# A retention layer with a SoLU feed-forward layer: steps of 256 tokens and four heads, attention on 64x64 tiles, and a fixed order for every engine

## The chip, the cores and the metric

The kernel runs on one core of one Trainium2 chip. The metric is the device time of one execution in microseconds (us), the median of several runs, each kernel measured in turn with the kernel before on the same chip. Ratios are the mean time of one kernel's fast runs divided by the mean time of the fast runs of the kernel before in the same rounds, so they are not quite the ratio of the medians that are quoted beside them. "Span" is the time from the first to the last instruction in a profiled execution; it is some 2 us shorter than the run's time for most kernels here.

Engine names: PE is the matrix engine, DVE the vector engine, ACT the scalar engine, POOL the third element-wise engine, SP the engine that issues most DMA transfers.

## The reference

Shortened to what is computed:

```python
def _attn_ref(q, k, v):                        # q, k, v: (8 batches, 8 heads, 576 tokens, 64) float32
    scores = (1 / sqrt(64)) * q @ k.T
    gamma = 1.0 - 2.0 ** (-5.0 - arange(8))    # one decay per head
    Dmat = where(rel >= 0, gamma ** rel, 0)    # rel = query position - key position
    return (scores * Dmat) @ v

def _moe_ref(x, w_in, w_out, g_ln):            # x: (4608 tokens, 512), w_in (512, 1024), w_out (1024, 512)
    h = x @ w_in
    solu = h * softmax(h)
    ln = (solu - mean) / sqrt(var + 1e-06) * g_ln
    return ln @ w_out
```

There is no softmax in the attention, so it can be computed as a recurrence: within a chunk of 128 tokens the masked scores are formed, and what earlier chunks contribute goes through a 64x64 state for each head. The 4608 tokens are 36 chunks of 128.

## The kernel before

Each of 36 steps takes one chunk of 128 tokens and all eight heads. The parts that the change touches:

```python
def load(i):                       # q, k, v: one token per partition
    ...
    nc.sync.dma_start(out=t, in_=src[b, :, c * P : (c + 1) * P, :].rearrange("h p d -> p h d"))

def qk_tp(i):                      # 8 transpositions of 128x128 into ONE PSUM bank (tqk)
    ...
def scores(i):                     # 8 matmuls, 64 rows x 128 columns, two at a time
    for hp in range(4):
        for e in range(2):
            dd = slice(e * 64, e * 64 + 64)
            nc.tensor.matmul(out=s_ps[:, e, hp], lhsT=qkT[dd, 1, hp], rhs=qkT[dd, 0, hp], ...)
def kv_mm(i):                      # 8 matmuls, 128 rows x 64 columns: new state
    ...
def inter(i):                      # 4 matmuls 128x128: query times the old state
    ...
def av(i):                         # 8 matmuls, 128 rows x 64 columns: scores times v
    ...
def mm1(i):                        # 8 matmuls: h = x @ w_in, two PSUM banks, one buffer
    ...
def mm2(i):                        # 8 matmuls: o = ln @ w_out, one PSUM bank, one buffer
    ...
for i in range(-LEAD, NS + LAG):   # one hand-written software pipeline; order of issue = order of this text
    a = i + LEAD
    load(i + 6) ...
    state(a - 1); mask(a - 1); stats(i - 1); cast_v(a + 1); scale_qk(a + 1); rstd(i - 1)
    mm1(i); exp_(i); solu(i)
    qk_tp(a); qk_ev(a)
    mm2(i - LAG); o_ev(i - LAG)
    ln_tp(i - 1); ln_ev(i - 1)     # 8 transpositions into the SAME bank as tqk (tln)
    inter(a - 1); scores(a); av(a - 1); x_ev(a - 1); kv_mm(a)
    if i == -1: prep_w_in(); keep_warm(WARM1)
    if 0 <= i < LAG: prep_w2(i)    # w_out times g_ln, minus its column mean
```

Names in the profile: `h_ps` is the output of mm1, `o_ps` of mm2, `s_ps` of the scores, `tqk` and `tln` the transpositions, `e_sb` of the exponential, `solu` of the product h times exp(h), `w2g` and `w2c` the steps of w_out's preparation. I count the mm1 groups from 0 to 35.

The softmax here doesn't subtract the row's maximum and nothing guards it: scores larger than these inputs give would overflow.

## Time and profile before

Three runs gave 246.12 us (245.96 to 247.88).

| what | value | where it is read |
|---|---|---|
| first mm1 (0) starts, its second half starts | 20.84, 24.88 us | timeline of PE |
| mm1 5 starts | 60.69 us | timeline of PE |
| mean period of mm1, steps 10 to 30 | 5.498 us | timeline of PE |
| mm1 35 (the last) to the end | 19.8 us | timeline of PE, span |
| span | 243.4 us | page |

The overview of the kernel before, its span cut into 40 slices of 6.1 us; a digit is the busy share in tenths, and the fourth line counts the DMA packets:

```profile
PE   8375485779999999999999999999999999999861
DMA  8999999990889887979888978797788762111123
GB/s 167 218 367 218 263 292 219 184 209 28 178 192 196 191 209 160 224 157 206 189 197 181 212 160 213 175 240 175 174 205 193 172 169 46 43 46 74 57 86 86
DMA packets 120922, 42.42 MB, mean 174 GB/s; under 512 B 114624, under 2 KB 114752, under 8 KB 120896
```

For the first nine slices PE is idle for about a third of the time while the DMA engines are full, at only 167 to 367 GB/s; from the tenth slice to the end PE is full. Part 3 of the page of the kernel before gives the loads' queue (packets, MB, share of the 16 engines' span):

```profile
q1 hardware_dynamic: 120464, 41.96, 76.5%
```

So there are three stages with different limits: a start of 60 us, a steady stage bound by PE, and a tail. The busy time by window of the kernel before (columns: window, its length, then busy us of PE, PE's weight loads, DVE, ACT, POOL, the granted PE clock, the DMA share, GB/s) says the same:

```profile
core 0: us, PE busy (x) PEld busy (x) DVE busy (x) ACT busy (x) POOL busy (x), PEclk, DMA share, GB/s
0.00:20.00 20.00, 13.37 (x107) 6.98 (x108) 6.53 (x13) 7.20 (x11) 9.28 (x20) 0.75 1.13 245
20.00:40.00 20.00, 11.47 (x104) 5.77 (x103) 11.31 (x18) 9.73 (x17) 10.68 (x17) 0.91 1.15 257
60.00:200.00 140.00, 139.66 (x1491) 82.92 (x1488) 116.76 (x176) 103.24 (x152) 109.29 (x192) 1.00 0.84 191
```

In 140 us of the steady stage PE lacks 0.3 us; the other engines have 17 to 26% to spare. There a gain has to come out of PE's own time. One steady step on PE in the kernel before (columns: start, length, engine, line, operation, output and inputs, tile, shape, count):

```profile
128.75 1.89 PE L344 MATMUL o_ps<-w2c_105,lnT 128*128 128x512 f16 x8
130.57 0.61 PE L329 MATMUL tln<-ident,solu 128*128 128x128 f16 x8
131.01 0.39 PE L255 MATMUL av_ps<-qkT,sbd_109 128*128 128x128 f16 x4
131.33 0.40 PE L191 MATMUL s_ps<-qkT 64*128 64x128 f16 x8
131.66 0.41 PE L267 MATMUL av_ps<-ret,v_1975 128*64 128x128 f16 x8
131.90 0.29 PE L217 MATMUL kv<-v_2089,k_2092 128*64 128x64 f16 x8
132.13 1.90 PE L285 MATMUL h_ps<-w_in_103,xT 128*128 128x512 f16 x8
```

The ends that the profile gives overlap the next start (130.64 against 130.57 in the first two lines), so one reads the distances between starts. From the 128*128 tiles to the scores' 64*128, from there to 128*64, and from there back to 128*128 the tile mode changes: three changes a step.

The start, the first mm1 groups on PE in the kernel before (in brackets: how long PE had been idle just before, and what ended that):

```profile
20.84 1.03 PE L285 MATMUL h_ps<-w_in_103,xT 128*128 128x512 f16 x4
24.88 1.38 PE L285 MATMUL h_ps<-w_in_103,xT 128*128 128x512 f16 x4 [3.01 <-DVE w_in_103 L371]
```

The second half of the first mm1 waits 3.01 us for a cast of w_in on DVE. And the end, the last eviction of an output tile and the issue of its stores, in the timeline of the kernel before:

```profile
238.63 0.69 ACT L352 ACTIVATE o_sb<-o_ps,rs 128x512 f32<-128x512 f32 x1 [2.11 <-PE o_ps L344]
239.34 1.11 SPq L360 DMA_DIRECT2D out_dram<-o_sb  x2
```

### The profile page before, as it was taken

How to read it: one execution, taken by the hardware profiler on the slowest of the kernel's cores; microseconds unless marked ns; L12 is line 12 of the kernel's file. 1: busy time of each engine (PE TensorE's matmuls, PEld its weight loads, DVE VectorE, ACT ScalarE, POOL GpSimd, SP SyncE). 2: the span in 40 equal slices, each digit the busy share in tenths (PEclk: the TensorE clock that was granted, in tenths of full speed). 3: DMA queues.
4: the chain of work that ended last, by engine and by line, in shares of the span. 5: the costliest groups of instructions: out<-in, count | busy, mean ns of one | idle time of the engine just before them, and what ended most of it. 6: DMA issues, size and time to landing. Idle time of an engine off the chain costs nothing.

```text
span 243.4 us, 5629 instructions
## 1 busy us (share of the span) xinstructions
PE 215.8 (89%) x2138; PEld 123.6 (51%) x2138; DVE 174.1 (72%) x266; ACT 156.7 (64%) x230; POOL 155.0 (64%) x277
## 2 busy tenths in 40 slices
PE   8375485779999999999999999999999999999861
PEld 2252233445555655566555655565655555554420
DVE  1450777599979888977798889887888898876400
ACT  2143557547666777777776777777776677766631
POOL 8243575176957888788578887886678878721200
PEclk9858979989999999999999999999999999999998
DMA  8999999990889887979888978797788762111123
GB/s 167 218 367 218 263 292 219 184 209 28 178 192 196 191 209 160 224 157 206 189 197 181 212 160 213 175 240 175 174 205 193 172 169 46 43 46 74 57 86 86
DMA packets 120922, 42.42 MB, mean 174 GB/s; under 512 B 114624, under 2 KB 114752, under 8 KB 120896
## 3 DMA queue, kind: packets, MB, share of 16 engines
q1 hardware_dynamic: 120464, 41.96, 76.5%
q8 instruction: 16, 0.26, 0.5%
q10 hardware_dynamic: 432, 0.12, 0.2%
q14 instruction: 10, 0.08, 0.1%
HBM read 32.63 MB, written 9.44 MB: 173 GB/s over the span
## 4 chain that ended last, share of the span: by engine, by line
PE 73%; SPq 10%; DVE 7%; ACT 5%; DMA 2%; issue 1%; ACTq 0%
PE h_ps L285 25%; PE o_ps L344 24%; SPq L94 7%; PE tln L329 7%; PE tqk L173 5%; PE av_ps L267 4%; PE s_ps L191 4%; PE av_ps L255 2%; DVE solu L301 2%; DVE w2c_105 L386 2%; DMA w_f<-in_moe_w_out_dram 2%; ACT w2g_104 L374 2%; ACT o_sb L352 1%; PE kv L217 1%; ACT e_sb L295 1%
## 5 line engine op out<-in xcount | busy, mean ns | idle before, releaser
L285 PE MATMUL h_ps<-w_in_103,xT 128*128 128x512 f16 x288 | 71.2, 389 | 3.6 <-DVE w_in_103 L371 3.0
L344 PE MATMUL o_ps<-w2c_105,lnT 128*128 128x512 f16 x288 | 68.0, 379 | 2.8 <-ACT o_sb L352 2.8
L295 ACT ACTIVATE e_sb<-h_ps 128x1024 f32<-128x1024 f32 x36 | 36.8, 1023 | 49.6 <-PE h_ps L285 49.6
L301 DVE TENSOR_TENSOR solu<-h_ps,e_sb 128x1024 f16<-128x1024 f32 x36 | 43.7, 1215 | 9.2 <-ACT e_sb L295 9.2
L309 DVE BATCH_NORM_STATS2 bs<-solu 128x6 f32<-128x512 f16 x72 | 45.9, 680 | 0.1
L202 DVE TENSOR_TENSOR ret<-s_ps,masks 128x1024 f16<-128x1024 f32 x36 | 43.7, 1215 | 2.1 <-PE s_ps L191 2.1
L285 PEld LDWEIGHTS <-xT 128*128 128x128 f16 x288 | 26.1, 99 | 34.3 <-issue 8.3
L344 PEld LDWEIGHTS <-lnT 128*128 128x128 f16 x288 | 26.9, 98 | 30.0 <-issue 3.6
L181 ACT COPY qkT<-tqk 128x1024 f16<-128x1024 f16 x36 | 36.1, 1004 | 8.1 <-PE tqk L173 8.1
L337 ACT COPY lnT<-tln 128x1024 f16<-128x1024 f16 x36 | 36.1, 1004 | 2.1 <-PE tln L329 2.1
L352 ACT ACTIVATE o_sb<-o_ps,rs 128x512 f32<-128x512 f32 x36 | 24.7, 687 | 17.3 <-PE o_ps L344 13.9
L237 POOL TENSOR_TENSOR gt<-tt,small 128x256 f32<-128x256 f32 x24 | 14.7, 613 | 26.0 <-DVE tt L236 26.0
L329 PEld LDWEIGHTS <-solu 128*128 128x128 f16 x288 | 19.0, 97 | 15.8 <-issue 11.5
L329 PE MATMUL tln<-ident,solu 128*128 128x128 f16 x288 | 21.8, 218 | 5.0 <-ACT qkT L181 5.0
L276 ACT CAST xT<-av_ps 128x512 f16<-128x512 f32 x36 | 21.5, 596 | 3.4 <-PE av_ps L267 3.4
L236 DVE TENSOR_TENSOR tt<-kv,gt 128x256 f32<-128x256 f32 x24 | 10.1, 422 | 15.4 <-PE kv L217 8.9
L191 PE MATMUL s_ps<-qkT 64*128 64x128 f16 x288 | 14.7, 223 | 4.3 <-ACT qkT L181 4.3
L318 POOL TENSOR_SCALAR w<-se 128x1 f32<-128x1 f32 x36 | 10.3, 285 | 4.8 <-ACT e_sb L295 1.5
L191 PEld LDWEIGHTS <-qkT 64*128 64x128 f16 x288 | 8.3, 96 | 8.4 <-ACT qkT L181 5.2
L242 POOL CAST sbd_109<-gt 64x256 f16<-64x256 f32 x8 | 3.1, 394 | 10.2 <-DVE gt L233 9.9
L233 DVE TENSOR_TENSOR gt<-kv,small 128x256 f32<-128x256 f32 x8 | 3.4, 424 | 8.3 <-PE kv L217 8.3
L366 PE MATMUL wm<-zeros 128*128 128x512 f16 x18 | 7.4, 593 | 1.2 <-DVE zeros L126 1.2
(509 smaller groups left out, 303.1 us busy)
## 6 DMA issues: line engine op xcount, KB each, us to landing
qr<-in_q_dram SPq DMA_DIRECT2D x32, 256.0 KB, 3.7
kr<-in_k_dram SPq DMA_DIRECT2D x32, 256.0 KB, 4.4
vr<-in_v_dram SPq DMA_DIRECT2D x32, 256.0 KB, 4.4
out_dram<-o_sb SPq DMA_DIRECT2D x32, 256.0 KB, 2.2
w_in_f<-in_moe_w_in_dram SPq DMA_DIRECT2D x4, 512.0 KB, 5.6
w_f<-in_moe_w_out_dram SPq DMA_DIRECT2D x4, 512.0 KB, 5.4
qr<-in_q_dram SPq DMA_DIRECT2D x8, 128.0 KB, 4.0
kr<-in_k_dram SPq DMA_DIRECT2D x8, 128.0 KB, 3.7
```

The lines of the kernel that those rows point to most:

```text
L181: nc.scalar.copy(out=qkT, in_=d["tp"])
L191: nc.tensor.matmul(out=s_ps[:, e, hp], lhsT=qkT[dd, 1, hp], rhs=qkT[dd, 0, hp], start=True, stop=True,)
L202: nc.vector.tensor_tensor(out=ret, in0=d["s"].rearrange("p e h j -> p (e h) j"), in1=masks[:, m].unsqueeze(1).to_broadcast([P, 8, P]), op= ...
L276: nc.scalar.copy(out=xT, in_=d["av"])
L285: nc.tensor.matmul(out=h_ps[:, hh], lhsT=d["xT"][:, dc], rhs=w_in16[:, dc, hh], start=(dc == 0), stop=(dc == 3),)
L295: nc.scalar.activation(out=e_sb, in_=d["h"], func=ACT.Exp, accum_out=se)
L301: nc.vector.tensor_tensor(out=s16, in0=d["h"], in1=d["e"], op=ALU.mult)
L309: nc.vector.bn_stats(out=bs[:, half], in_=d["solu"][:, half * 512 : half * 512 + 512])
L329: nc.tensor.transpose(out=tp[:, c], in_=d["solu"][:, c * P : (c + 1) * P], identity=ident)
L337: nc.scalar.copy(out=lnT, in_=d["ltp"])
L344: nc.tensor.matmul(out=o_ps, lhsT=d["lnT"][:, c], rhs=w2c16[:, c], start=(c == 0), stop=(c == 7))
L352: nc.scalar.activation(out=o_sb, in_=d["o"], func=ACT.Copy, scale=d["rs"])
```

## The change

Its intent: fewer and larger DMA packets, one tile mode for all three small attention products, and on every engine an order that was found by a simulation beforehand instead of the order of the program text. A step is now 256 tokens and four heads (two attention steps make two chunks of 128 tokens for the feed-forward part, so there are 36 steps again). Cut to its core:

```diff
-                    out=t, in_=src[b, :, c * P : (c + 1) * P, :].rearrange("h p d -> p h d")
+                out=t, in_=src[b, hh, 256 * wi : 256 * wi + 256, :].rearrange(
+                    "h (p j) d -> p h j d", j=2            # two tokens of 64 numbers: 512 bytes in a row
+                ),
 ...
-        for hp in range(4):                                # scores, 8 matmuls of 64x128 tiles
-            for e in range(2):
-                    out=s_ps[:, e, hp], lhsT=qkT[dd, 1, hp], rhs=qkT[dd, 0, hp],
+        for hp in range(2):                                # scores, 16 matmuls of 64x64 tiles
+            for j in range(2):
+                for c in range(2):
+                    for e in range(2):
+                            out=sv[ee[c], e, hp, j], lhsT=qkT[ee[e], 1, hp, j, ee[c]],
+                            rhs=qkT[ee[e], 0, hp, :, ee[c]], start=True, stop=True,
 ...                                                        # AV and KV likewise: 16 matmuls of 64x64 tiles
-        nc.vector.tensor_copy(out=v16, in_=d["vr"])        # cast of v on DVE
+        nc.gpsimd.tensor_copy(out=t, in_=st[i]["vr"])      # on POOL
 ...
-    for i in range(-LEAD, NS + LAG): ...                   # hand-written pipeline
+    FIRST = dict(ACT="qe0 qe1 wi3a xe0 ...", DVE=..., PE="K0 T0 S0 T1 I0 V0 S1 K1 T2 ... T3 M1_0 I2 ...",
+                 POOL=..., SP="ldk0 ldv0 ldq0 ldq1 ldk1 lwi3 ...")   # orders of the first steps, as found by search
+    PER = 5.36                                             # later steps: position in a period
+    start, done = order_ops(ops, caps)                     # static simulation of all engines
+    for o in sorted(ops, key=lambda o: start[o.name]):
+        o.emit()
```

In these orders T is a transposition of q and k, S the scores, V the product with v, K the state product, I the product with the old state, M1 and M2 the large products, L the second transposition. The casts `sq`, `sk`, `cv` of q, k and v and the state casts `sc` stand on POOL; `rs` is the LayerNorm factor.

## The prediction

> **What bounds it now** (busy time by window, PE timeline, chain of waits).
> - 60 to 219 us: PE, busy 20.0 of every 20 us at clock 1.00; DVE has 16 to 17, ACT 14 to 15, POOL 15 to 17. The h_ps matmuls start every 5.34 to 5.57 us, mean 5.50. Of that mm1 + mm2 + two transposes are 1.73+1.73+0.45+0.45 = 4.36; small attention matmuls and gaps are 1.1.
> - 0 to 60 us: start. PE works 40 of 60 us. DMA is saturated (share above 1.0 to 50 us) at 187 to 303 GB/s; 114,624 of 120,922 packets are under 512 B. Orders make it worse: DVE sits 7.54 us on a vr load before it casts w_in, so half of the first mm1 starts only at 24.9 us; mm1 6 starts at 60.7.
> - 219 to 243 us: tail. mm2 and o_ev alternate on one PSUM bank, 2.8 us a step; the last mm1 starts at 223.6, the end is 19.8 us later.
>
> **What the change does.**
> 1. Two tokens a partition make q, k, v rows 512 B instead of 256. The skill's page "DMA: Bandwidth & Descriptors" (Specifications) puts line rate at 512 B and up; the 367 GB/s slice of before, in which weights load, is my stand-in. Estimate: DMA share falls from 76% to 45%. It pays only at the start: in steady state DMA waits are nil.
> 2. Scores, AV and KV run as 16 matmuls each on 64x64 tiles, four at a time instead of eight, two at a time. Streaming time stays (0.22, 0.22, 0.11 us); what goes is mode changes: three modes followed one another with gaps near 0.1 us; now all three share one ("TensorEngine Tiling (Array Packing)", Key Properties: a mode change drains the array). Estimate: attention 1.1 to 0.97, step 5.50 to 5.36; over 36 steps 5 us.
> 3. V casts go from DVE (0.4 to 0.8 us) to POOL, rstd's small ops half to DVE. POOL about 4.5 us a step, DVE 4.65, ACT 4.5: 84 to 87% of PE.
> 4. Orders: loads interleaved by need, w_in casts not behind a v load, evictions of the one transpose bank hidden behind mm1 and mm2. Tail unchanged in kind, one mm2 fewer after the last mm1: 4 us less.
>
> **Sum.** Before the first mm1, 3 MB of q, k, v and 2 MB of w_in at about 350 GB/s: 14 us + 2.5, so mm1 0 at 17 us. Steps 0 to 4 are held by ACT and DVE (eight w2g casts, 5 us; eight w2c, 5.4): 5.2 each, 26. Then 28 steps at 5.37, 150; last two at 4.5, 9. Last mm1 at 202, end 15.5 later: span 218; launch adds 2.
>
> **Predicted: 220 us, 8 in 10 within 212 to 229. Faster by over 2%: 0.95; within 2%: 0.03; slower: 0.02.** Of 26 us about 16 come from the start, 5 from the steady steps, 4 from the tail.
>
> **Right or wrong in the profile.** Packets under 512 B gone, early GB/s above 300; mm1 0 near 17, mm1 6 near 49 us; h_ps period 5.3 to 5.4 with PE busy 20 of 20; scores, AV and KV without gaps; last mm1 to end 15 to 16 us.
>
> **What would make it wrong.** 64x64 tiles limited by issue (48 small matmuls with weight loads a step), giving 5.6 and more; POOL at 84% in a fixed order stalling PE; low clock at the start (before: 0.50 at 10 to 20 us) with fewer warm-up matmuls; 512 B packets short of 350 GB/s.

What is called "mm1 6 starts at 60.7" and "mm1 6 near 49 us" there is misnumbered by one: the group at 60.69 us in the kernel before is mm1 5. The sum of the prediction puts mm1 5 at 17 + 26 = 43 us.

## The result

The kernel after took 230.8 us (230.4 to 230.96, 4 runs), the kernel before 247.0 us (245.96 to 248.11, 4 runs) in the same rounds. The ratio is 0.934, with a 95% interval of 0.929 to 0.940. It is clearly faster, by 16 us. The prediction had 220 us and a range of 212 to 229, so the size was wrong.

| us from the start of the span | before | predicted | after |
|---|---|---|---|
| mm1 0 | 20.84, rest 24.88 | 17 | 19.21, rest 20.91 |
| mm1 5 | 60.69 | 43 | 51.65 |
| mm1 5 to mm1 33 | 154.0 | 150 | 150.9 |
| mm1 33 to mm1 35 | 8.9 | 9 | 8.9 |
| mm1 35 to the end | 19.8 | 15.5 | 17.4 |
| span | 243.4 | 218 | 228.9 |

Of the 14.5 us by which the span fell, 9.0 lie before mm1 5, 3.1 between mm1 5 and mm1 33, and 2.4 in the tail. Against the prediction, mm1 5 is 8.65 us late and the tail 1.9 us long; the rest of the sum holds to within a microsecond.

The overview of the kernel after, read as that of before (slices of 5.7 us):

```profile
PE   7577587998989999999999999999999999999961
DMA  7999999783992355999776866877855442222243
GB/s 189 329 351 254 299 316 289 207 244 77 282 333 61 103 128 135 272 312 296 196 203 180 210 185 184 240 212 196 224 128 132 122 98 66 63 57 49 47 102 83
DMA packets 66659, 42.64 MB, mean 186 GB/s; under 512 B 5056, under 2 KB 60480, under 8 KB 66624
```

Of the packets under 512 B 5056 are left, where there were 114,624, and the DMA engines are still full for seven slices, to 40 us. They move more per second than before, but 254 to 351 GB/s, not steadily the 350 that the prediction had. Part 3 of the page of the kernel after (queue, packets, MB, share of the 16 engines' span):

```profile
q1 hardware_dynamic: 66192, 41.96, 66.8%
```

The bytes are the same and the packets 45% fewer, yet the share fell only from 76.5 to 66.8%, of a span 14.5 us shorter. The prediction had 45%. (That did not follow from its own rate: 41.96 MB at 350 GB/s are 120 us, 55% of its span of 218.)

The busy time by window of the kernel after:

```profile
0.00:20.00 20.00, 14.19 (x178) 7.65 (x179) 9.75 (x26) 7.35 (x10) 13.63 (x23) 0.74 1.01 282
20.00:40.00 20.00, 14.22 (x220) 8.14 (x219) 14.25 (x25) 14.88 (x23) 13.59 (x22) 0.91 1.04 297
60.00:200.00 140.00, 139.37 (x2130) 85.36 (x2130) 117.18 (x205) 106.95 (x157) 106.20 (x171) 1.00 0.66 181
```

In the first 40 us no compute engine is full: over the two windows ACT, DVE, POOL and PE are busy for 56, 60, 68 and 71%. Only the DMA engines are full (share 1.01 and 1.04).

One steady step on PE in the kernel after:

```profile
130.17 0.61 PE L461 MATMUL tln<-ident,solu 128*128 128x128 f16 x8
130.62 0.28 PE L295 MATMUL xy<-qkT,sbd_125 128*128 128x128 f16 x2
130.73 0.27 PE L295 MATMUL xy<-qkT,sbd_128 128*128 128x128 f16 x2
130.94 0.42 PE L330 MATMUL s_ps<-qkT 64*64 64x128 f16 x16
131.19 0.39 PE L295 MATMUL xy<-ret,v_2718 64*64 64x128 f16 x16
131.41 0.29 PE L295 MATMUL xy<-v_2853,k_2808 64*64 64x64 f16 x16
131.63 1.90 PE L475 MATMUL o_ps<-w2c_120,lnT 128*128 128x512 f16 x8
```

From the scores' start to the next group's start it is now 0.25 us, where it was 0.33; the change of tile mode between scores and AV is gone, and twice the number of matmuls on quarter tiles costs no more time. Also, the transposition tln follows its predecessor at once. In the kernel before it waited about 0.09 us in each step for the eviction of tqk from the one bank that both use (it started at 130.57, and mm2, which started at 128.75, holds PE for 1.73 us, the distance from mm1's start at 132.13 to the next group's). The mean period fell from 5.498 to 5.327 us.

The start on PE in the kernel after:

```profile
19.21 1.00 PE L412 MATMUL h_ps<-w_in_118,xT 128*128 128x512 f16 x2
20.91 1.46 PE L412 MATMUL h_ps<-w_in_118,xT 128*128 128x512 f16 x6 [0.70 <-ACT w_in_118 L582]
...
25.70 1.89 PE L412 MATMUL h_ps<-w_in_118,xT 128*128 128x512 f16 x8
...
34.88 1.89 PE L412 MATMUL h_ps<-w_in_118,xT 128*128 128x512 f16 x8
```

The first three mm1 stand 6.5 and 9.2 us apart, where a steady step takes 5.33.

The end of the kernel after, the last mm2, its eviction and the last stores:

```profile
222.14 4.43 SPq L497 DMA_DIRECT2D out_dram<-o_sb  x8
222.16 1.89 PE L475 MATMUL o_ps<-w2c_120,lnT 128*128 128x512 f16 x8 [0.90 <-ACT o_sb L482]
224.14 0.69 ACT L482 ACTIVATE o_sb<-o_ps,rs 128x512 f32<-128x512 f32 x1 [2.03 <-PE o_ps L475]
```

The eviction ends at 224.83 and the span at 228.9: 4.1 us pass in storing. In the kernel before it was 4.1 us as well, from 239.32 to 243.4, though it has two stores where the kernel after has eight in this group of issues. The gain of 2.4 us comes from one mm2 fewer after the last mm1 (four instead of five): the last ones stood 2.80 us apart before, and the first of them now starts 0.44 us later after mm1 35, behind a transposition (2.17 instead of 1.73 us).

### The profile page after: what moved, and what is told of

It reads as the page before. It is cut to its first block, busy times and chain, and to the rows that moved or that the text cites. A ratio compares the mean times of both kernels' runs of the same rounds, so it can differ in the third digit from the quotient of the medians.

```text
span 228.9 us, 7317 instructions
## 1 busy us (share of the span) xinstructions
PE 208.0 (91%) x2964; PEld 122.9 (54%) x2964; DVE 170.7 (75%) x307; ACT 157.6 (69%) x230; POOL 150.9 (66%) x243
## 2 busy tenths in 40 slices
DMA packets 66659, 42.64 MB, mean 186 GB/s; under 512 B 5056, under 2 KB 60480, under 8 KB 66624
## 3 DMA queue, kind: packets, MB, share of 16 engines
q1 hardware_dynamic: 66192, 41.96, 66.8%
## 4 chain that ended last, share of the span: by engine, by line
PE 70%; DMA 9%; DVE 6%; POOL 5%; ACT 4%; SPq 2%; issue 2%; ACTq 0%; POOLq 0%; DVEq 0%
PE o_ps L475 24%; PE h_ps L412 22%; PE xy L295 8%; DMA qr<-in_q_dram 6%; PE tln L461 6%; PE tqk L275 6%; PE s_ps L330 4%; DMA kr<-in_k_dram 3%; DVE solu L432 2%; DVE ret L363 2%; SPq L243 1%; POOL g L385 1%; DVE bs L438 1%; ACT o_sb L482 1%; ACT qkT L283 1%
## 5 line engine op out<-in xcount | busy, mean ns | idle before, releaser
L412 PE MATMUL h_ps<-w_in_118,xT 128*128 128x512 f16 x288 | 68.6, 380 | 1.0 <-ACT w_in_118 L582 0.7
L425 ACT ACTIVATE e_sb<-h_ps 128x1024 f32<-128x1024 f32 x36 | 36.8, 1024 | 20.5 <-PE h_ps L412 20.3
L482 ACT ACTIVATE o_sb<-o_ps,rs 128x512 f32<-128x512 f32 x36 | 24.8, 688 | 23.7 <-PE o_ps L475 14.5
L385 POOL TENSOR_TENSOR g<-tt,small 128x128 f32<-128x128 f32 x48 | 19.6, 409 | 25.7 <-DVE tt L381 25.3
L400 ACT CAST xT<-xy 128x512 f16<-128x512 f32 x36 | 21.4, 595 | 2.6 <-DVE g L377 1.5
L381 DVE TENSOR_TENSOR tt<-xy,g 128x128 f32<-128x128 f32 x48 | 13.7, 286 | 7.6 <-ACT xT L400 3.8
L330 PE MATMUL s_ps<-qkT 64*64 64x128 f16 x576 | 15.6, 228 | 2.8 <-ACT qkT L283 2.8
L330 PEld LDWEIGHTS <-qkT 64*64 64x64 f16 x576 | 9.8, 110 | 6.2 <-ACT qkT L283 3.7
L377 DVE TENSOR_TENSOR g<-xy,small 128x128 f32<-128x128 f32 x16 | 4.6, 287 | 6.5 <-PE xy L295 4.8
L442 DVE BATCH_NORM_AGGREGATE mv<-bs 128x2 f32<-128x12 f32 x36 | 7.5, 209 | 1.2
L588 ACT ACTIVATE w2g_119<-w_f,gln 128x512 f16<-128x512 f32 x8 | 5.4, 716 | 2.5 <-DMA w_f<-in_moe_w_out_dram 2.4
L425 ACT ACTIVATION_READ_ACCUMULATOR e_sb<-h_ps 128x1 f32 x36 | 7.0, 194 | 0.0
```

What stands on the lines that cost most here:

```text
L330: nc.tensor.matmul(out=sv[ee[c], e, hp, j], lhsT=qkT[ee[e], 1, hp, j, ee[c]], rhs=qkT[ee[e], 0, hp, :, ee[c]], start=True, stop=True,)
L385: nc.gpsimd.tensor_tensor(out=d["g"][:, c], in0=d["tt"], in1=g128(i % 2), op=ALU.mult)
L412: nc.tensor.matmul(out=h_ps[:, hh], lhsT=st[2 * w + dc // 2]["xT"][:, c, dc % 2], rhs=w_in16[:, dc, hh], start=(dc == 0), stop=(dc == 3),)
L425: nc.scalar.activation(out=d["e"], in_=d["h"], func=ACT.Exp, accum_out=ws[w]["se"][:, c : c + 1])
L482: nc.scalar.activation(out=d["osb"], in_=d["o"], func=ACT.Copy, scale=ws[t // 2]["rs"][:, t % 2 : t % 2 + 1])
```

## Experiments

Seventeen kernels were run. Medians are of fast runs; two of the six runs of e5 and one of b2 were slow and are left out. The kernel before, measured beside them, had medians from 245.9 to 248.0 us, so between groups of runs the ratios are the safer comparison. "Wrong" means that the result is false but the amount of work on each engine is kept, except for what the edit names. Theories: A is that the loads are slower than predicted, B that the start is held by work and waits among the engines, C that the PE clock is.

### e1_rows2k: the same bytes in 2 KB rows (wrong)

```diff
-                out=t, in_=src[b, hh, 256 * wi : 256 * wi + 256, :].rearrange("h (p j) d -> p h j d", j=2)
+                out=t, in_=flat[65536 * i : ...].rearrange("(p h j d) -> p h j d", p=P, h=4, j=2)   # 2 KB per partition
```

> Wrong result on purpose: q, k and v are read as the same bytes in the same number of DMAs, but as 2 KB rows per partition, so no packet of 512 B is left. In the changed kernel mm1 0 starts at 19.2 us, mm1 5 at 51.65, the time is 230.8. Theory A (data comes late, because 512 B packets run at some 260 to 290 GB/s and not at 350): the start gets faster, mm1 5 at about 46 us, the time about 225. Theory B (the loads are not the limit; orders and chains of single engines are): mm1 5 stays at 50 us or later, the time at 229 or more. In steady state both expect h_ps every 5.30 us as now.

Measured: 225.41 us (ratio 0.9135), span 223.3. mm1 0 at 18.13, mm1 5 at 47.38. The overview's GB/s line of this run:

```profile
GB/s 213 395 361 384 386 359 159 201 83 223 356 134 141 132 148 262 304 259 213 201 224 172 221 182 160 231 191 191 195 159 140 130 86 56 45 54 50 59 95 84
```

From the second to the sixth slice it moves 359 to 395 GB/s. What follows: with the orders as they are, packets of 512 B were 4.3 us of the 8.65 us at mm1 5 (51.65 less 47.38). With the orders searched again it is less: between b2 and e14 below, the same edit moves mm1 5 by 1.3 us (47.82 to 46.53). The edit also changes the order of the addresses; that was not tested apart. The median time of a packet on its DMA engine was 18 ns for 256 B (before), 27 ns for 512 B (after) and 84 ns for 2 KB (here): 16 engines x 512 B / 27 ns is 303 GB/s, with 2 KB it is 390.

### e10_rows256: the kernel after with 256-byte rows (wrong)

```diff
-                out=t, in_=src[b, hh, 256 * wi : 256 * wi + 256, :].rearrange("h (p j) d -> p h j d", j=2)
+                out=t.rearrange("p h j d -> p (h j) d"),
+                in_=src[b, :, 256 * wi + P * hf : 256 * wi + P * hf + P, :].rearrange("h p d -> p h d"),
```

> Wrong result on purpose: in the changed kernel the same bytes of q, k and v are read as 256 B rows again (eight heads of 128 tokens instead of four heads of 256 tokens), all else unchanged. From the packet durations (18 to 21 ns for 256 B, 27 to 29 for 512 B) a load takes 1.3 us of all engines instead of 0.9. If the larger packets carry the gain of the start, mm1 5 goes from 51.65 to about 59 us and the time from 230.8 to 237 or more. If the orders carry it, mm1 5 moves by less than 3 us.

Measured: 240.09 us (ratio 0.972). mm1 5 at 56.91, period 5.327. So the larger packets alone are worth 9.3 us, 5.3 of them by mm1 5 and all by mm1 8 (79.31 against 69.86 us); the steady period is the same to a nanosecond. At mm1 8 this kernel is even behind the kernel before (77.03 us): without the larger packets the other changes show no gain up to there. The prediction gave the start the larger part, but did not split it between packets and orders.

### e2_noload: q, k and v loaded for two steps only (wrong)

```diff
+        if i >= 2:
+            st[i][nm + "r"] = st[i % 2][nm + "r"]
+            return
```

> Wrong result on purpose: q, k and v are loaded for the first two steps only and read again by all others, so only 4 MB of weights compete at the start. Theory A: mm1 0 at about 13 us (w_in casts) and the five steps to mm1 5 shrink from 32.4 us to about 26, as predicted; mm1 5 near 39, the time near 218. Theory B: mm1 0 moves just as far, but the five steps still take 30 us or more, so mm1 5 near 44 and the time near 223.

Measured: 226.35 us (ratio 0.917). mm1 0 at 19.59, mm1 5 at 49.03. With hardly any DMA after 20 us (3 GB/s from 20 to 40 us) it is not faster than e1, so the loads cannot be the whole of the miss: both runs meet another limit. For mm1 0 the trace names it: in PE's order mm1 0 stands behind the transposition of k of the fourth step, which waited for POOL's conversion of that k until 19.19 us. Theory A's figures for this run (mm1 0 at 13) were missed by far, and the expectation rested on the idea that nothing else would hold mm1 0.

### e3_nofirst: the searched start orders taken out

```diff
-FIRST = dict(ACT=(...), DVE=(...), PE=(...), POOL=(...), SP=(...))
+FIRST = {}
```

> The start orders found by search are taken out, and all engines follow the periodic key from the first step on (result correct). Theory A: the start is bound by bytes, which stay the same, so the time is within 2 us of 230.8. Theory B: the order of the start is what counts, so the time rises by 4 us or more. The period of h_ps stays at 5.30 us.

Measured: 236.03 us (ratio 0.957), right result. mm1 5 at 58.44 instead of 51.65, the period unchanged at 5.327. The start orders are worth about 5 us against the periodic order of the same kernel; the hand-written order of the kernel before was not tried. They, too, matter only at the start.

### e4_mode: two more changes of tile mode in each step

```diff
-        op(f"S{i}", "PE", "S", [f"qe{i}"], (i, 0.3), ...)      # scores after the product with the old state
+        op(f"S{i}", "PE", "S", [f"qe{i}"], (i, -0.05), ...)    # scores before it
```

> In every step after the first ten the scores come before inter instead of after it, which breaks up the run of 64x64 matmuls: two more mode changes a step, nothing else (result correct). If a mode change costs about 0.1 us of PE, as the gaps in the two traces suggest, the period of h_ps rises from 5.30 to about 5.45 to 5.50 and the time by 3.5 to 5 us. If mode changes are hidden and the gain of the steady state came from the order of the transposes alone, the period stays within 0.03 us and the time within 1 us.

The order in PE's timeline of this run, scores before the product with the old state:

```profile
132.92 0.42 PE L330 MATMUL s_ps<-qkT 64*64 64x128 f16 x16
133.27 0.40 PE L295 MATMUL xy<-qkT,sbd 128*128 128x128 f16 x4
133.60 0.42 PE L295 MATMUL xy<-ret,v 64*64 64x128 f16 x16
```

The groups now stand 0.35 and 0.33 us apart; in the kernel after the scores were followed after 0.25 us.

Measured: 235.12 us (ratio 0.952), right result; period 5.534, which is 0.207 more for two changes, so 0.10 us for one. mm1 5 stands at 52.28, near the 51.65 of the kernel after. This confirms the second step of the prediction: one change fewer is 0.10 of the 0.171 us that a step became shorter; the wait of tln for the bank, 0.09, covers the rest.

### e5_gln: g_ln loaded as 128 packets of 32 bytes (wrong)

The kernel loads g_ln with eight values for each partition that lie 128 apart, so 4 KB come as 1024 packets of 4 bytes.

```diff
-    in_=moe_g_ln.rearrange("(c p) -> p c", p=P)
+    in_=moe_g_ln.rearrange("(p c) -> p c", p=P)
```

> Wrong result on purpose (the gains are in the wrong order): the 4 KB load of g_ln is read as 128 rows of 32 B and no longer as 1024 packets of 4 B. In the changed kernel w_in chunk 1, behind which it is queued, lands 2.4 us after the load ahead of it, and w_out chunk 1 4.2 us after the last recorded landing, where 1.4 and 2.2 would do. Theory A1 (most of the lateness of the loads is this one load, not the rate of 512 B packets): mm1 5 goes from 51.65 to about 48.5 us and the time from 230.8 to about 228. Theory A2 (it is the rate of 512 B packets, 285 GB/s in the trace against 350 assumed): mm1 5 by less than 1 us, the time by less than 1 us.

Measured in five rounds: the four fast runs have a median of 228.56 us (228.07 to 229.07), ratio 0.928 (0.922 to 0.934). That is 2.2 us less than the kernel after by the medians and 1.5 by the ratios, between the two expectations; the two intervals overlap (0.929 to 0.940 for the kernel after), so it is not clear of noise. The profiled run fell in the slow state, its first load of q came 0.85 us later than in the kernel after, and its mm1 5 at 51.7 is not compared.

### e6_now2: e1 without the preparation of w_out (wrong)

```diff
-        for x in (c, c + 1):
-            op(f"wg{x}", "ACT", ...)           # eight casts on ACT, with the matmuls of the column mean
-    for x in range(8):
-        op(f"wc{x}", "DVE", ...)               # eight subtractions on DVE
+        nc.vector.memset(w2c16, 0.03)
```

> Wrong result on purpose: on top of the run with 2 KB rows (mm1 0 at 18.13, mm1 5 at 47.38 us, time 225.4) the preparation of w_out is taken out (eight casts on ACT, eight matmuls for the mean, eight centrings on DVE; mm2 reads a constant). Theory B1 (with the data in time, the rest of the miss is w_out's preparation standing in the chain: ACT casts ahead of lnT and the transposes): mm1 0 stays near 18, the five steps to mm1 5 shrink from 29.3 us to 26 or less, mm1 8 from 64.2 to about 59, the time to about 220. Theory B2 (the steps are held by q/k/v conversion on POOL and the turns of PE, ACT and DVE through single buffers): the five steps stay above 28, the time above 223.5.

Measured: 228.26 us (ratio 0.928), slower than e1 although it does less. mm1 5 at 50.43. The reason is in PE's timeline of this run, of which these are two mm1 groups:

```profile
18.30 3.50 PE L407 MATMUL h_ps<-w_in,xT 128*128 128x512 f16 x8
37.72 3.62 PE L407 MATMUL h_ps<-w_in,xT 128*128 128x512 f16 x8
```

Two mm1 took 3.50 and 3.62 us, where all others take 1.89: the granted clock was down, at 0.50 from 11.3 to 21.6 and from 35.2 to 42.0 us. The Trainium skill, "TensorE: Matmul & The Clock Gate" (Part 1), puts the clock at half after an idle window of about 3.4 us. The nearly doubled times agree with the half; but PE was not idle throughout such a window, it was busy for 1.62 of the 3.40 us before the clock fell the second time. In e1 mm1 0 was slow too (2.95 us), the fourth mm1 was not: there the matmuls of w_out's mean, which look like a cost, had kept the clock up. So the run does not answer its question, and e8 repeats it.

### e7_warm and e8_now2w: the clock held up by idle matmuls

e7 is the kernel after with 20 matmuls on zeros before the first mm1 (right result). e8 is e6 with 38 of them.

```diff
+        fill = dict(K0=3, T0=4, T1=2, V0=1, S1=2, K1=1, T2=4, V1=1, S2=1, T3=1)     # e7; e8 has T4, L0, M1_2, L1 as well
         for o in sorted(ops, key=lambda o: start[o.name]):
             o.emit()
+            for _ in range(fill.get(o.name, 0)):
+                nc.tensor.matmul(out=wm, lhsT=zeros[:, :P], rhs=zeros, start=True, stop=True)
```

> Correct result: 20 dummy matmuls fill PE's idle time before the first mm1, so that the granted clock does not fall (0.50 from 10 to 20 us in the changed kernel). Theory C (the low clock costs the start): mm1 0 runs at full speed and the time falls by 1.5 us or more. If PE at the start only waits for POOL and for loads, mm1 0's own 2.9 us may shrink by 1 us, and the time falls by less than 1 us.

> Wrong result on purpose: the run without w_out's preparation and with 2 KB rows again, now with 38 dummy matmuls in PE's idle time up to the first mm2, because in that run the granted clock fell and two mm1 took 3.5 and 3.6 us. If the low clock hid the gain of the missing preparation (B1): the five steps from mm1 0 to mm1 5 take 26 to 27 us (29.3 with the preparation, 32.1 without it at the low clock), mm1 5 at 44.5 or earlier, the time 222 or less. If the steps are held by POOL and the single buffers (B2): the five steps stay above 28 us.

Measured: e7 231.21 us (ratio 0.939) at a mean granted clock of 0.993: no gain over the 230.8 of the kernel after (ratio 0.934), so theory C falls for this kernel. The test is not complete, since the clock was still 0.50 from 20.6 to 24.0 us, within mm1 0; mm1 5 stands at 50.91. e8 225.07 us (225.04 to 225.22, ratio 0.909), mm1 0 at 18.36 and mm1 5 at 47.32, which are five steps of 29.0 us. That is where e1 stood with w_out's preparation in it (47.38). The casts `w2g` on ACT and `w2c` on DVE, which the prediction had named as what holds these steps, cost nothing in sum there. They do hold the third mm1 (31.26 us in e1, 29.74 in e8), but the fourth is late again (36.06 in e1, 36.69 in e8), behind the state cast on POOL that e11 looks at. Of the idle matmuls in e8 only those before the second mm1 can have delayed it, by about 0.5 us at most: it follows them at once, and the product that frees its buffer ended at 24.07 us; it starts at 24.61.

### e9_halfpool: half of POOL's conversion of q and k in steps 3 to 11 (wrong, on e8)

```diff
-            out=t..., in0=st[i][nm + "r"], in1=g_of(i, base), op=ALU.mult,
+            out=t...[:, hs], in0=st[i][nm + "r"][:, hs], in1=g_of(i, base)[:, hs], op=ALU.mult,   # two of four heads
+        if 3 <= i <= 11: nc.vector.memset(t[:, :, 2:4], 0.0)
```

> Wrong result on purpose: the run before last with 2 KB rows, no w_out preparation and a held clock, in which PE still waited for POOL eight times up to mm1 5; now POOL converts only two of four heads of q and k in steps 3 to 11 (0.5 us less for each of 18 operations; DVE zeroes the rest). Theory B2a (POOL's conversions in their fixed order hold the start): the five steps from mm1 0 to mm1 5 go from 29.0 us to 27 or less, mm1 5 to about 45.5, the time from 225.1 to about 223. Theory B2b (it is the turns of PE, ACT and DVE through single buffers, xy, tp, s and h, and POOL only comes last by a little): the five steps stay above 28.3 us.

Measured: 225.14 us (ratio 0.911), mm1 5 at 46.95, five steps 28.5 us. The amount of work on POOL in these steps is not what holds them either; 0.5 us is all that it gives. (POOL's work before mm1 0 is left as it was.)

### e11_rs0: one operation moved in POOL's order (on e8)

The trace of e8 shows POOL's state cast behind `rs`, which waits for statistics from DVE:

```profile
31.83 0.69 POOL L450 TENSOR_TENSOR rs<-w,small 128x2 f32<-128x2 f32 x1 [0.29 <-DVE w L444]
32.47 0.85 POOL L389 CAST sbd<-g 64x256 f16<-64x256 f32 x2
```

```diff
-        "... sk6 rs0 sc4 cv5 sq7 sq6 sm5 sc5 cv6 sq8 ..."
+        "... sk6 sc4 cv5 sq7 sq6 sm5 sc5 cv6 rs0 sq8 ..."
```

> Base: the run with 2 KB packets, no w_out preparation and a warm clock (mm1 0 at 18.36, mm1 3 at 36.69, mm1 5 at 47.32, time 225.1). Here one operation moves: the first rstd (rs0) stands behind the v cast of step 6 in POOL's order, so the state casts of step 4 no longer stand behind an operation that waits for the LayerNorm statistics. Theory D1 (POOL's order, rs0 before the state cast, holds step 2 to 3): mm1 3 at about 35.4, mm1 5 at about 46.0, time about 223.9. Theory D2 (the single bank of h, or PE's own order, holds it): mm1 3 at 36.4 or later, mm1 5 within 0.4 us of 47.3, time within 0.4 us of 225.1.

Measured: mm1 3 at 35.70 (it was 36.69) and mm1 5 at 46.34 (47.32): in the trace theory D1 holds for 1.0 us. The median of 224.91 us (224.14 to 226.51, ratio 0.911) does not show it; the runs scatter by more than that.

### e12_hfree and e13_all: freeing the h buffer earlier (wrong)

```diff
-        nc.vector.tensor_tensor(out=d["solu"], in0=d["h"], in1=d["e"], op=ALU.mult)
+        nc.vector.tensor_tensor(out=d["solu"], in0=d["e" if t < 10 else "h"], in1=d["e"], op=ALU.mult)
```

> Same base. For the first ten tiles of 128 tokens the product after exp reads exp's result twice instead of h and exp's result (wrong on purpose, same size), so the one PSUM bank pair of h is free as soon as exp has read it, about 1.2 us earlier in each turn. Theory D2 (turn mm1, exp, product, mm1 through the one h buffer holds the first steps): the five steps from mm1 0 to mm1 5 fall from 29.0 to 26.5 or less, mm1 5 at 45.0 or earlier, time at most 223. Theory D1 and D3 (PE's order with its waits for the state casts and the one transposition bank): five steps at 28.3 or more, time within 0.6 us of 225.1.

> Same base, with the three relaxations together: half of POOL's q and k conversion in the early steps, rs0 behind the v cast of step 6, h free after exp (wrong on purpose). If D1, D2 and POOL's amount are the only holders left between mm1 0 and mm1 5, the five steps take 26 us or less (what I had predicted) and the time is about 222. Theory D3 (PE's fixed order through the one transposition bank and the one bank of scores): five steps still 28 or more, time 224.5 or more.

Measured: e12 took 229.5 us (ratio 0.927), slower than e8 by 4.4 us, which neither theory had. e13 took 224.92 us (ratio 0.909), five steps 27.7 us, between its two expectations. The edit, which is in both, had a side effect that I had not thought of. DVE and POOL in the trace of e12:

```profile
22.85 1.68 DVE L427 TENSOR_TENSOR solu<-e_sb 128x1024 f16<-128x1024 f32 x1
...
23.41 1.38 POOL L380 TENSOR_TENSOR g<-tt,small 128x128 f32<-128x128 f32 x1
```

The same two instructions in the trace of e8:

```profile
22.85 1.22 DVE L427 TENSOR_TENSOR solu<-h_ps,e_sb 128x1024 f16<-128x1024 f32 x1
...
23.41 0.40 POOL L380 TENSOR_TENSOR g<-tt,small 128x128 f32<-128x128 f32 x1
```

They start at the same times, but DVE's took 1.22 and POOL's 0.40 us. The product had read h from PSUM and its exponential from SBUF; now both operands come from SBUF. The Trainium skill, "SBUF — State Buffer" (Who interferes with whom), says that such a DVE instruction contends with a POOL instruction that reads SBUF, and that the loser blocks. The two lines agree: POOL's operation of 0.40 us was held until about the time that DVE's ended; and DVE's, 0.46 us longer than before, had started while POOL was still converting k, from 22.41 to 23.45. Nor is the product slow by itself with both operands in SBUF: of the ten in e12 four took 1.22 us as before, the others 1.32 to 2.03. So e12 measures a collision along with the h buffer, and the question stayed open.

### b1_tail: mending what the profile showed (right result)

```diff
+TAIL = (33, 35)
-        d["o"] = pools["o"].tile([P, DM], FP, tag="o", name="o_ps")
+        if t in TAIL:                                      # the last mm2 use two banks in turn
+            d["o"] = pools["s"].tile([P, 2, DM], FP, tag="s", name="o_ps")[:, 0]
+        else: ...
-                    nc.sync.dma_start(                     # last store
+                    (nc.scalar if j and t >= NT - 1 else nc.sync).dma_start(
-    in_=moe_g_ln.rearrange("(c p) -> p c", p=P)            # 4-byte packets
+    in_=moe_g_ln.rearrange("(p c) -> p c", p=P)            # w_out read likewise, w_in's columns permuted in its cast
 ...                                                       # early memsets shared by POOL and DVE
```

> Correct result, start orders unchanged. Three repairs: g_ln and w_out are read with eight neighbouring rows per partition (no 4-byte packets; columns of w_in permuted in its cast), the zeroing of the state tiles is shared between POOL and DVE, and at the end the mm2 of tiles 33 and 35 use the free bank of the scores, half of the last store goes through ACT's queue. From the run with g_ln alone 1.8 us; at the end two waits of 1.0 us and about 1 us of issue: from the start of the last mm1 to the end 17.4 becomes 14.5. Together about 226 us against 230.8 for the changed kernel.

Measured in five rounds: 226.5 us (225.43 to 227.14), ratio 0.914 (0.910 to 0.918). The last mm1 to the end is 14.7 us instead of 17.4. The result is right, and it beats both kernels, the kernel after by 4.3 us.

### b2_search: b1 with start orders searched again (right result)

The search was given the durations of the loads as the trace shows them, and 25 idle matmuls were added; the edit replaces the lists in FIRST.

> Correct result: as the run before, with the start orders searched again in a static model that has the durations of loads as the trace shows them (0.92 us per 256 KB, landing 2.5 us after its turn, 0.9 us lost to the first constants) and 25 dummy matmuls that hold the clock. If the start is limited by orders that were found for loads that come too early, another 2 us: about 224. If the order has nothing left to give once the loads are as they are, it equals the run before within 1 us.

Measured: five fast runs with a median of 226.16 us (225.49 to 228.61), ratio 0.917 (0.911 to 0.922): the same as b1 within the noise. mm1 5 comes at 47.82, 2.8 us earlier than in b1, but most of this is given back: 1.6 us are left at mm1 8 (66.78 against 68.42), 1.0 at mm1 35 (209.07 against 210.09), and the tail is 0.4 us longer. The clock, too, was up in b2 (0.50 from 8.4 to 25.5 us in b1, 1.00 in b2), so the 2.8 us are not the orders' alone. This search found little more to gain.

### e14_best and e15_h2: the h buffer, without the collision (wrong, on b2)

e14 is b2 with the 2 KB rows of e1. e15 is e14 with two h buffers of one PSUM bank each: both halves of mm1 write the same bank, and exp and the product read that bank twice, so all engines do the same work and the product still reads one operand from PSUM.

```diff
-    CAP = dict(..., h=1, ...)
+    CAP = dict(..., h=2, ...)
-        h_ps = pools["h"].tile([P, DFF], FP, ...);  out=h_ps[:, hh]
+        h_ps = pools["h"].tile([P, 512], FP, ...);  out=h_ps
-        tk[t]["h"] = h_ps
+        tk[t]["h"] = h_ps.unsqueeze(1).to_broadcast([P, 2, 512])
```

> The version with searched start orders (rs0 late, the first product before the fourth mask; in its own run mm1 0 at 20.32, mm1 5 at 47.82, so five steps 27.5, time 226.8), with q, k and v read as 2 KB packets (wrong on purpose); w_out's preparation is in. Theory D2 (with orders free of needless waits, what keeps five steps from 26 us is the turn mm1, exp, product, mm1 through one h buffer, plus PE's own work): mm1 0 near 18.6, five steps 27.0 to 27.6, mm1 5 at about 46, time 222 to 223. Rival (late loads made up the rest even in that version): five steps at most 26.2, mm1 5 at most 44.9, time at most 221.5.

> The same with two h buffers of one PSUM bank each instead of one buffer of two banks: both halves of mm1 go to the same bank, exp and the product read that bank twice (wrong on purpose, same work on every engine, the product still reads one operand from PSUM). Theory D2: five steps at most 26.3, at least 0.8 us less than with one buffer, time 0.5 to 1.5 us less. Rival (PE's order, its waits for conversions and the one transposition bank hold the steps, not h): five steps within 0.4 us of the run with one buffer, time within 0.4 us.

Measured: e14 225.06 us (224.03 to 226.43, ratio 0.911), five steps 27.7 us; e15 224.43 us (223.96 to 225.14, ratio 0.908), five steps 27.4 us. In the profile of e15 everything comes 1.3 us later from mm1 0 on, so only distances are compared. With two buffers the first three steps take 16.1 instead of 17.4 us, and the next two give most of it back (11.3 instead of 10.2, with PE waiting for a q conversion from POOL). So the rival holds for the steps: the single h buffer is not what keeps five steps from 26 us. (The median of e15 is 0.6 us lower, but the runs of the two overlap.) Nor was the time of e14 the 222 to 223 that I had expected.

## Why the prediction was wrong in size and right in kind

**Right: what bounds the steady stage, and its gain.** The prediction had the 28 steps at 5.37 us; they took 150.9 us, 5.39 each, and the mean period in steps 10 to 30 is 5.327. Its reasons hold: a mode change costs 0.10 us (e4), one in each step is gone, and the wait of tln for the shared bank is gone as well. The Trainium skill, "TensorEngine Tiling (Array Packing)" (Key Properties), says that a change of tiling mode drains the engine; it names no time, and e4 measures it. The feared limit of 48 small matmuls did not show: a group of 16 on 64x64 tiles takes 0.22 to 0.25 us from start to start. DVE, ACT and POOL have more room than was predicted: in the window of 140 us, which is 26.3 steps, they are busy 4.5, 4.1 and 4.0 us a step.

**Right: where the gain lies.** Most of it is at the start (9.0 of 14.5 us), and it comes from the packets (9.3 us when undone alone, e10) and the orders (5 us when replaced by the periodic order, e3). The two are not to be added: each was undone with the other in place, and one may shorten what the other waits for.

**Wrong: "3 MB of q, k, v and 2 MB of w_in at about 350 GB/s: 14 us + 2.5, so mm1 0 at 17 us".** This step failed by its rate. The prediction took 512 B for full rate, from the Trainium skill's "DMA: Bandwidth & Descriptors" (Specifications) and from a slice of the kernel before at 367 GB/s. But 2.09 of the 2.23 MB of that slice were in packets of 4 KB, those of w_in; it was a stand-in for the weights, not for q, k and v. Packets of 512 B took 27 ns, and the kernel after moved 282 and 297 GB/s in its first two windows of 20 us. With the orders as they were this is 4.3 of the 8.65 us (e1), with orders searched again 1.3 (b2 and e14). Another 1.5 to 2.2 us of run time, not clear of noise, go to the 4-byte packets of g_ln, which the prediction had not seen (e5). These are still there in e1, so they are not part of its 4.3 us; whether the two add was not tested. The rate also explains a part of the DMA share, 66.8% instead of 45%. The prediction had listed "512 B packets short of 350 GB/s" as what would make it wrong; the range did not allow for it.

Even at 359 to 395 GB/s mm1 0 came at 18.1 to 18.4, not 17, and there the step failed in its path as well: it let mm1 0 start when the loads are in. PE's timeline in e1:

```profile
17.73 0.61 PE L270 MATMUL tqk<-ident,k 128*128 128x128 f16 x4 [0.39 <-POOL k L253]
18.13 2.95 PE L407 MATMUL h_ps<-w_in,xT 128*128 128x512 f16 x8
```

The transposition that stands before mm1 0 in PE's order waited for POOL's conversion of k, and mm1 0 follows it at once; it did not wait for w_in. The chain of waits from the first q, which landed at 6.1 us, to 17.7 us is POOL's for 9.4 us: conversions of q, k and v and the state casts, one after the other. In the kernel after the first two matmuls of mm1 0 start behind the same conversion (19.21), and only the rest waits 0.70 us for a cast of w_in, which had waited for its transfer. The prediction had feared "POOL at 84% in a fixed order stalling PE", but for the steady stage. This is read from traces; no run shortens POOL's work before mm1 0.

**Wrong: "Steps 0 to 4 are held by ACT and DVE (eight w2g casts, 5 us; eight w2c, 5.4): 5.2 each, 26".** It is the reasoning of a steady stage, put on a stage that is not steady. The table of windows shows no compute engine full there, and with w_out's preparation taken away mm1 5 came at the same place (e8 at 47.32, e1 at 47.38), though the third mm1 came 1.5 us earlier. With fast loads the five steps took 29.3 us in e1. What the runs put in its place is a chain of waits that changes hands: moving one LayerNorm factor behind POOL's state casts gave 1.0 us (e11), halving POOL's conversions 0.5 us (e9), the version with newly searched orders 1.6 us (five steps 27.7 in e14 against 29.3 in e1; it holds the changes of b1 and a higher clock as well), a second h buffer at most 0.3 us (e15). Each relaxation lets the next wait appear; no run brought the five steps under 27.3 us. Which of the remaining waits would have to go together to reach 26 stays open; it was not shown that 26 can be reached at all. The clock is not it: in e8, at a mean granted clock of 0.995, the five steps took 29.0 us.

**Wrong by a little: the tail.** The prediction had 15.5 us, and it was 17.4. One mm2 fewer was right; the term that was mis-sized is its worth, "4 us less". It was 2.4: an mm2 in the tail took 2.80 us, as the prediction itself had said, and 0.44 us were lost again before the first of them. The end of the last eviction to the end of the span, 4.1 us in both kernels, did not change. b1 shows that the tail can be 14.7 us.

The terms add up: 8.65 us late at mm1 5, 0.9 in the 28 steps, -0.1 in the last two, 1.9 in the tail make the 11.4 us between the 217.5 us of the unrounded sum and the 228.9 us of the span.

## What to carry to other kernels

A rate for DMA is to be read from packets of the size that the new kernel will have: median time of a packet times count over 16 engines, not GB/s of a slice that moves something else. A stage in which no engine is full is not bounded by anyone's busy time; walk its waits in order of time, and expect that taking one away yields a part of what the idle time suggests, since the next wait stands close behind. When an experiment takes work away, check that it has not taken something useful with it: with w_out's matmuls gone the granted clock fell to 0.50 (e6), and an operand moved from PSUM to SBUF made two engines collide.

## What the Trainium skill lacked or had wrong

- "DMA: Bandwidth & Descriptors" (Specifications) gives 512 B as the least transfer for line rate. Here packets of 512 B took 27 ns (303 GB/s on 16 engines, 282 to 297 in windows of the kernel after), packets of 2 KB 84 ns (390 GB/s). Between them lie 4.3 us at mm1 5 (e1), 1.3 with orders searched again (e14).
- The same table gives about 358 GB/s as the limit of memory for one core. With 2 KB packets slices of e1 show 359 to 395 GB/s. This is no contradiction: further down the page says that the figure holds with both cores of a memory domain streaming, and here one core runs.
- That page explains why small descriptors are slow, with 256 B as its example, but not what a load in 4-byte pieces costs a kernel. 1024 packets of 4 B for one 4 KB vector cost 1.5 to 2.2 us of run time, not clear of noise (e5).
- "TensorEngine Tiling (Array Packing)" (Key Properties) says that a mode change drains, without a time. It is 0.10 us here (e4), and groups of 16 matmuls on 64x64 tiles took no longer than 8 on 64x128 tiles (0.25 us to the next start, against 0.33 with a mode change in it).
- "TensorE: Matmul & The Clock Gate" (Part 1) gives an idle window of about 3.4 us as what halves the clock, but not how much work a window may hold. In e6 the clock fell at 35.2 us after 3.40 us in which PE was busy for 1.62. The half itself agrees (3.50 and 3.62 us for mm1 instead of 1.89), and "SBUF — State Buffer" agrees with e12 (0.40 us on POOL became 1.38).
